# Sigmoid attention and a top-128 routed feed-forward on one core: small broadcasts on another queue, and several operations at another place in the order

## The chip, the core and the metric

The kernel runs on one core of a Trainium2 chip. The core has a matrix engine (TensorE, PE in the profile, with its weight loads as PEld), a vector engine (VectorE, DVE), an activation engine (ScalarE, ACT), GpSimd (POOL) and a SyncE (SP), which here only issues transfers. Each engine works through its own list of instructions in order. The metric is the device time of one execution in microseconds, as the median of several runs.

## What is computed

Attention first, for 8 batches and 12 heads, with 448 tokens and 64 values a head, all in float32. There is no softmax: each score passes a sigmoid.

```python
scores = (q @ k.T) / sqrt(64) - log(448)
x = sigmoid(scores) @ v             # heads side by side: 8 x 448 x 768
```

Then, in each batch, a gate picks 128 of the 448 tokens, and only these go through a feed-forward of width 1024. All other rows are copied.

```python
s = x[b] @ w_gate                   # one score a token
top = the 128 tokens with the highest s
h = relu(x[b, top] @ w1)            # w1 768 x 1024
out[b, top] = x[b, top] + sigmoid(s[top])[:, None] * (h @ w2)   # w2 1024 x 768
```

## The kernel before

**Stages and units.** Four heads of one batch are a group. There are 24 groups, three to a batch, and two groups make a stage, so there are 12 stages, s = 0 to 11, and a last one, s = 12, that holds only what is left over. A stage has seven units, n = 0 to 6; (s, n) below is unit n of stage s. `unit(s, n)` computes a block of scores on TensorE (line 214) and its sigmoid on ScalarE (line 222). `gap(s, n)` is called after each unit and fills the time with other work: the attention values of the stage before (line 249) in four parts, the first at (s-1, 6) and the others at (s, 0), (s, 1) and (s, 2), and after the third unit, pieces of the feed-forward (lines 382 and 392). TensorE runs this list in the written order.

**Order.** The order of instructions on every engine is that in which the Python code emits them; no scheduler moves them. `late` is a table from (s, n) to work that is emitted there, filled by `routed(b)`.

**Turning.** `turn(i)` (lines 189 to 196, VectorE) transposes the raw keys and queries of group i. It is emitted at (s, 5) for the first group of the next stage and at (s, 1) for the second group of its own. Raw buffers, kT and qT are two deep. `load(i)` fetches the raw data of a group and `load_v(s)` the values of a stage in eight transfers (lines 115 and 117), all on SyncE. The values' buffer is two deep too: `load_v(s+1)` is emitted at (s, 0), and its first transfer waits until TensorE has done with the values of stage s-1, at the end of (s, 2).

**Picking the tokens.** A batch b passes through these steps:
- `take` (line 264, VectorE) transposes the attention result out of PSUM into x_b, and `gate_part` (lines 272 and 275) multiplies by w_gate and sums.
- `gate(b)` (lines 288 to 307) adds up the scores into `total`, writes them to DRAM (`scores`) and reads them back into all 128 partitions (`rep`).
- `ranking(b)` (lines 315 and 318, then `place`) counts for each token how many others are above it, writes the counts (`ranks`) to DRAM, and reads them back to all partitions (`spot`).
- `choose(b)` (line 341 to 354, in `select`) compares `spot` with the partition's number and so finds which token stands at which place. The row numbers drive an indirect gather of the rows `xe` from DRAM (line 352, GpSimd).
- `follow(b)` transposes xe on TensorE (`turn_rows`, line 366) and queues three pieces of `ffn1` and three of `ffn2`. The last ffn2 piece scatters the rows to the output (line 398, GpSimd).
- `store(b)` writes x_b to DRAM in four transfers (line 281) and `copy_out(b)` copies all rows of the batch to the output (line 284), both on SyncE.

The small transfers scores, rep, ranks and spot are issued by GpSimd. For batch 0 the steps stand at: gate (2, 2), store (2, 4), ranking (3, 1), copy_out (3, 3), choose (4, 0), follow (4, 3). For batch 1: gate (3, 3), store (3, 4), ranking (4, 1), choose (5, 0), follow (5, 3). The other batches follow in the same pattern, two batches in three stages.

**Weights.** `WEIGHTS` says after which unit SyncE issues the loads of w1 (six transfers of 512 KB) and w2 (eight of 384 KB): five of w1 after (1, 5), the sixth and four of w2 after (2, 5), and the last four of w2 after (3, 1).

**A wait for a lane.** Each transfer signals one of eight semaphores of its queue in turn. In the built program a transfer therefore also waits for the one that used the same semaphore eight transfers earlier.

Of the kernel before, what the change touches and what calls it, by code (L numbers as in the profile page):

```python
# [10 lines left out]
I32 = mybir.dt.int32  # L11
AF = mybir.ActivationFunctionType
ALU = mybir.AluOpType
# [4 lines left out]
def kernel(  # L18
# [11 lines left out]
    nc = tc.nc  # L30

    B, H, S, Dh = q.shape
    D = H * Dh
    F = moe_w1.shape[1]
    CAP = moe_capacity
    P = 128
    TT = 32
    TB = S // TT
    NF = 3
# [4 lines left out]
    NU = 2 * NF + 1  # L44
    HP = H // 2
    KD = D // P
    KF = F // P
    ND = D // 3
# [7 lines left out]
    assert Dh == 2 * TT and TB == HK + 2 and S == TT * TB and H == 4 * NG and NQ == 2 * NS  # L56
    assert D == KD * P and F == KF * P and KF % 4 == 0 and 0 < CAP < S and D == HP * P

    out_flat = out.rearrange("b s d -> (b s) d")

    const = ctx.enter_context(tc.tile_pool(name="const", bufs=1))
    raw = ctx.enter_context(tc.tile_pool(name="raw", bufs=2))
# [5 lines left out]
    moe = ctx.enter_context(tc.tile_pool(name="moe", bufs=1))  # L68
# [7 lines left out]
    def banks(which):  # L76
        if which == "any":
            turns[1] ^= 1
            which = "psc" if turns[1] else "o"
        if which == "psc":  # L80
            return ps_sc.tile([P, 2, 512], F32, name="psc")
        if which == "o":
            turns[0] ^= 1
            which = turns[0]
        return ps_o[which].tile([P, 2, 512], F32, name=f"o{which}")
# [4 lines left out]
    def load(i):  # L90

        if i >= NQ:
            return
        raws[i] = [raw.tile([P, TB * Dh], F32, name=f"raw_{nm}") for nm in "kq"]
        for t, src in zip(raws[i], (k, q)):
            nc.sync.dma_start(
                out=t, in_=bass.AP(tensor=src.tensor, offset=src.offset + i * 4 * S * Dh,
                                   ap=[[TB * Dh, P], [1, TB * Dh]]))
# [19 lines left out]
                              in_=blocks(4 * (n // 2), HK + n % 2, 4, 1))  # L118


    WEIGHTS = {(1, NU - 2): (0, 5), (2, NU - 2): (5, 10), (3, 1): (10, KD + KF)}
    w1_sb = const.tile([P, KD, F], F32, name="w1_sb")
    w2_sb = const.tile([P, KF, D], F32, name="w2_sb")

# [99 lines left out]
    x_tiles, gate_parts, st = {}, {}, {}  # L224
# [43 lines left out]
    def gate_part(i):  # L268
        b, g = divmod(i, NG)
        for hp in range(2 * g, 2 * g + 2):  # L270
            tmp = moe.tile([P, TB, TT], F32, name="scr")
            nc.vector.tensor_tensor(  # L272
                out=tmp, in0=x_tiles[b][:, :, hp, :],
                in1=wg_b[:, hp:hp + 1, :].to_broadcast([P, TB, TT]), op=ALU.mult)
            nc.vector.tensor_reduce(out=gate_parts[b][:, :, hp], in_=tmp, axis=AX.X, op=ALU.add)  # L275
# [10 lines left out]
    def gate(b):  # L286

        nc.vector.tensor_reduce(out=gate_s[:, :TB], in_=gate_parts[b], axis=AX.X, op=ALU.add)
        by_dim = moe.tile([P, TT], F32, name="by_dim")
        nc.vector.transpose(by_dim, gate_s)  # L290
        parts = moe.tile([TT, 4, TT], F32, name="parts")
        for a in range(4):
            nc.vector.tensor_copy(parts[:, a], by_dim[a * TT:(a + 1) * TT])
        total = moe.tile([TT, TT], F32, name="total")
        nc.vector.tensor_reduce(out=total, in_=parts.rearrange("p a t -> p t a"), axis=AX.X,
                                op=ALU.add)
        scores = dram.tile([TB, TT], F32, name="scores")
        nc.gpsimd.dma_start(out=scores, in_=total[:TB])
        rep = moe.tile([P, S], F32, name="rep", bufs=2)
        nc.gpsimd.dma_start(out=rep, in_=bass.AP(tensor=scores.tensor, offset=scores.offset,  # L300
                                                 ap=[[0, P], [1, S]]))
        by_token = moe.tile([TT, TT], F32, name="by_token")
        nc.vector.transpose(by_token, total)
        for m in range(4):
            n = min(NC, TB - m * NC)
            nc.vector.tensor_copy(score[m * TT:(m + 1) * TT, :n],
                                  by_token[:, m * NC:m * NC + n])
        st[b]["rep"] = rep
# [13 lines left out]
    def place(b):  # L322

        nc.vector.tensor_add(place_s[:, :NC], above, level)
        by_col = moe.tile([P, TT], F32, name="by_col")
        nc.vector.transpose(by_col, place_s)
        ranks = dram.tile([P, TT], F32, name="ranks")
        nc.gpsimd.dma_start(out=ranks, in_=by_col)
        spot = moe.tile([P, 4, NC * TT], F32, name="spot")
        nc.gpsimd.dma_start(  # L330
            out=spot, in_=bass.AP(tensor=ranks.tensor, offset=ranks.offset,
                                  ap=[[0, P], [TT * TT, 4], [1, NC * TT]]))
        st[b]["spot"] = spot.rearrange("p m c -> p (m c)")[:, :S]

    def select(b, s0, n):

        picked = []
        for what in (number.rearrange("p r t -> p (r t)"), st[b]["rep"]):
            got = moe.tile([P, 1], F32, name="got", bufs=4)
            junk = moe.tile([P, S], F32, name="scr")  # L340
            nc.vector.scalar_tensor_tensor(
                out=junk[:n], in0=st[b]["spot"][:n], scalar=slots[s0][:n], in1=what[:n],
                op0=ALU.is_equal, op1=ALU.mult, accum_out=got[:n, 0:1])
            picked.append(got)
        row = moe.tile([P, 1], I32, name="row", bufs=2)
        nc.vector.tensor_copy(row[:n], picked[0][:n])
        idx = moe.tile([P, 1], I32, name="idx", bufs=2)
        nc.vector.tensor_scalar_add(idx[:n], picked[0][:n], float(b * S))
        gt = moe.tile([P, 1], F32, name="gate", bufs=2)
        nc.scalar.activation(gt[:n], picked[1][:n], AF.Sigmoid)  # L350
        xe = moe.tile([P, D], F32, name="xe", bufs=2)
        nc.gpsimd.indirect_dma_start(
            out=xe[:n], out_offset=None, in_=st[b]["x_d"][:, :],
            in_offset=bass.IndirectOffsetOnAxis(ap=row[:n, 0:1], axis=0))
        st[b].update(idx=idx, gate=gt, xe=xe)
# [31 lines left out]
    def ffn2(b, n, part, where):  # L387
        ps = banks(where)[:, 0]
        xe = st[b]["xe"]
        cols = slice(part * ND, (part + 1) * ND)  # L390
        for t in range(KF):
            nc.tensor.matmul(ps[:n, :ND], st[b]["hT"][:, t, :n], w2_sb[:, t, cols],  # L392
                             start=(t == 0), stop=(t == KF - 1))
        nc.vector.scalar_tensor_tensor(  # L394
            out=xe[:n, cols], in0=ps[:n, :ND], scalar=st[b]["gate"][:n, 0:1],
            in1=xe[:n, cols], op0=ALU.mult, op1=ALU.add)
        if part == D // ND - 1:
            nc.gpsimd.indirect_dma_start(
                out=out_flat[:, :],
                out_offset=bass.IndirectOffsetOnAxis(ap=st[b]["idx"][:n, 0:1], axis=0),  # L400
                in_=xe[:n], in_offset=None)


    ready = []

    def routed_groups(b, n):
        for f0 in range(0, KF, 3):
            ready.append((ffn1, (b, n, f0, min(f0 + 3, KF))))
        for part in range(D // ND):
            ready.append((ffn2, (b, n, part)))  # L410

    def go(where="o"):
        if ready:
            fn, args = ready.pop(0)
            fn(*args, where)

    late = {}

    def put(where, s, n, fn, *args):
        where.setdefault((s, n), []).append((fn, args))  # L420

    def due(where, s, n):
        for fn, args in where.pop((s, n), []):
            fn(*args)

    def routed(b):

        s = (NG * b + NG - 1) // 2 + 1
        put(late, s, 4, store, b)
        if s == NS:  # L430
            return
        put(late, s + 1, 1, ranking, b)
        put(late, s + 1, 3, copy_out, b)
        if s + 2 <= NS:
            put(late, s + 2, 0, choose, b)
            put(late, s + 2, 3, follow, b)

    def ranking(b):
# [13 lines left out]
    def gates(i):  # L452
        gate_part(i)
        b, g = divmod(i, NG)
        if g == NG - 1:
            st[b] = {}
            gate(b)

    def gap(s, n):
        if n < 3 and s > 0:  # L460
            values(s - 1, n + 1)
            if n == 2:
                turns[0] = 1
                gates(2 * s - 2)
        if 3 <= n < NU - 1:
            if not ready:
                due(late, s, n)
            go("any" if s == NS else "o")
            if n == NU - 2 and s < NS - 4 and len(ready) > 1:
                go()  # L470
        if n == NU - 1 and s < NS:
            values(s, 0)
        due(late, s, n)
        if n == 3 and s > 0:
            gates(2 * s - 1)

    def stream():
        for b in range(B):
# [13 lines left out]
        for s in range(NS):  # L492
            for n in range(NU):
# [7 lines left out]
                if n == NU - 2:  # L501
                    turn(2 * s + 2)
                    load(2 * s + 4)
                load_weights(*WEIGHTS.get((s, n), (0, 0)))

        for n in range(5):
            gap(NS, n)
# [50 lines left out]
```

## Time and profile before

| what | value |
|---|---|
| median of 3 runs (lowest to highest) | 477.78 us (475.13 to 478.36) |
| span of the profiled execution | 476.9 us |
| mean granted TensorE clock | 0.987 |
| busy DVE, ACT, POOL | 227.5, 185.1, 47.0 us |
| data moved | 72.74 MB, mean 153 GB/s |
| TensorE idle within 113.08 to 141.21 us, with clock | 28.13 - 23.07 = 5.06 us, clock 0.88 |

The profile names a transfer or operation by what it writes and reads, as in `rep<-scores`. An engine is busy while one of its instructions runs. The chain of waits goes back from the last instruction to whatever released each step. The table's last row comes from the busy times by stretch, for the stretch from the fourth unit of stage 4 to the end of its feed-forward pieces; the feed-forward of batch 0 lies in it.

### The profile page before, as it was taken

What the parts mean: (1) busy time and instruction counts of PE and PEld (TensorE: products, weight loads), DVE (VectorE), ACT (ScalarE), POOL (GpSimd) and SP (SyncE); (2) the same over time, 40 slices, a digit from 0 to 9 for tenths busy, and PEclk for the clock granted to TensorE, in tenths of its full rate; (3) what the DMA queues carried; (4) which work ended last, traced back from release to release, by engine and by line L of the source; (5) the groups of instructions that cost most, each with busy time, mean ns of one, the idle gap of its engine ahead of it and who ended that gap; (6) DMA issues with size and microseconds to landing.
All of it is one profiled execution on the core that took longest, in us unless ns stands there. A gap on an engine that the chain in (4) does not pass through costs nothing.

```text
span 476.9 us, 14574 instructions
## 1 busy us (share of the span) xinstructions
PE 457.0 (96%) x6582; PEld 299.7 (63%) x6582; DVE 227.5 (48%) x557; ACT 185.1 (39%) x245; POOL 47.0 (10%) x74
## 2 busy tenths in 40 slices
PE   8998989896999999999999999999999999999994
PEld 3473636353864684664774654755656738999993
DVE  4309087657322826666910844954454628540100
ACT  3856455653234425535344435455434520101010
POOL 9000000010000010001100011011010010220000
PEclk9999989998899999999999999999999999999999
DMA  8928688999912881697860892986822734722000
GB/s 267 206 80 216 241 194 198 265 356 177 313 36 93 184 180 42 143 232 170 200 238 3 184 183 57 271 147 138 263 69 34 148 97 72 211 60 67 34 0 33
DMA packets 118941, 72.74 MB, mean 153 GB/s; under 512 B 96288, under 2 KB 108768, under 8 KB 118624
## 3 DMA queue, kind: packets, MB, share of 16 engines
q1 hardware_dynamic: 115808, 61.35, 50.5%
q0 software_dynamic: 3072, 10.47, 9.7%
q8 instruction: 51, 0.84, 0.7%
q14 instruction: 10, 0.08, 0.0%
HBM read 57.51 MB, written 25.31 MB: 174 GB/s over the span
## 4 chain that ended last, share of the span: by engine, by line
PE 85%; issue 4%; DMA 4%; DVE 3%; ACT 1%; SPq 0%; POOLq 0%; DVEq 0%; ACTq 0%
PE o L249 24%; PE psc L214 24%; PE o L382 14%; PE o L392 12%; PE psc L392 4%; PE psc L382 2%; PE o L214 2%; DMA rep<-scores 1%; DMA w_sb<-in_moe_w_dram 1%; ACT attn L222 1%; PE o L490 1%; PE o L366 1%; DMA out_dram<-xe,idx 1%; DVE x_b L264 1%; DVE scr L318 1%
## 5 line engine op out<-in xcount | busy, mean ns | idle before, releaser
L222 ACT ACTIVATE attn<-psc,bias_s 128x896 f32<-128x896 f32 x156 | 148.7, 1004 | 121.7 <-PE psc L214 121.6
L214 PE MATMUL psc<-qT,kT 32*64 32x448 f32 x2496 | 150.0, 544 | 4.2 <-ACT attn L222 4.2
L249 PE MATMUL o<-attn,raw_v 32*64 32x448 f32 x2304 | 135.4, 537 | 1.1 <-ACT o L252 1.1
L214 PEld LDWEIGHTS psc<-qT,kT 32*64 32x64 f32 x2496 | 61.0, 132 | 63.3 <-issue 40.1
L249 PEld LDWEIGHTS o<-attn,raw_v 32*64 32x64 f32 x2304 | 61.2, 133 | 51.4 <-issue 42.4
L264 DVE STREAM_TRANSPOSE x_b<-o 128x448 f32<-128x448 f32 x48 | 26.9, 618 | 98.1 <-PE o L249 98.1
L382 PEld LDWEIGHTS o<-xeT,w_sb 128*128 128x128 f32 x576 | 67.3, 196 | 10.0 <-issue 5.7
L382 PE MATMUL o<-xeT,w_sb 128*128 128x128 f32 x576 | 69.8, 281 | 0.9 <-ACT xeT L372 0.9
L392 PE MATMUL o<-w_sb,hT 128*128 128x256 f32 x272 | 62.5, 383 | 1.2 <-DVE xe L394 1.2
L392 PEld LDWEIGHTS o<-w_sb,hT 128*128 128x128 f32 x272 | 50.5, 190 | 15.6 <-issue 5.1
L189 DVE STREAM_TRANSPOSE kT<-raw_k 128x384 f32<-128x384 f32 x48 | 24.7, 553 | 35.1 <-PE psc L214 27.5
L394 DVE SCALAR_TENSOR_TENSOR xe<-o,gate,xe 128x256 f32<-128x256 f32 x17 | 8.2, 484 | 55.3 <-PE o L392 55.1
L275 DVE TENSOR_REDUCE gate_p<-scr 128x14 f32<-128x448 f32 x48 | 29.8, 621 | 1.6
L272 DVE TENSOR_TENSOR scr<-x_b,wg_b 128x448 f32<-128x448 f32 x48 | 29.5, 614 | 1.0
L385 ACT ACTIVATE hT<-o 128x384 f32<-128x384 f32 (+1 forms) x20 | 9.1, 454 | 50.3 <-PE o L382 50.3
L315 DVE TENSOR_SCALAR_CACHE_REDUCE scr<-rep,score 128x448 f32<-128x448 f32 (+1 forms) x32 | 21.5, 673 | 13.6 <-DMA rep<-scores 12.8
L249 PE MATMUL o<-attn,raw_h 32*64 32x448 f32 x384 | 27.2, 535 | 0.0
L392 PE MATMUL psc<-w_sb,hT 128*128 128x256 f32 x112 | 25.4, 380 | 0.0
L196 DVE STREAM_TRANSPOSE qT<-raw_q 128x896 f32<-128x896 f32 x23 | 24.7, 1073 | 0.7 <-DMA raw_q<-in_q_dram 0.7
L392 PEld LDWEIGHTS psc<-w_sb,hT 128*128 128x128 f32 x112 | 21.0, 190 | 3.4 <-issue 0.7
L318 DVE SCALAR_TENSOR_TENSOR scr<-rep,score,earlier 128x448 f32<-128x448 f32 (+1 forms) x32 | 21.8, 682 | 1.4
L252 ACT ACTIVATE o<-bias_s 1x1 f32<-1x1 f32 x36 | 5.9, 165 | 39.5 <-PE o L249 22.2
(69 smaller groups left out, 219.7 us busy)
## 6 DMA issues: line engine op xcount, KB each, us to landing
raw_k<-in_k_dram SPq DMA_DIRECT2D x24, 448.0 KB, 5.3
raw_q<-in_q_dram SPq DMA_DIRECT2D x24, 448.0 KB, 5.3
x_d<-x_b SPq DMA_DIRECT2D x32, 336.0 KB, 7.7
out_dram<-x_d SPq DMA_DIRECT2D x8, 1344.0 KB, 8.2
raw_v<-in_v_dram SPq DMA_DIRECT2D x48, 192.0 KB, 5.0
w_sb<-in_moe_w_dram SPq DMA_DIRECT2D x6, 512.0 KB, 7.9
w_sb<-in_moe_w_dram SPq DMA_DIRECT2D x8, 384.0 KB, 6.9
spot<-ranks POOLq DMA_DIRECT2D x8, 256.0 KB, 5.8
```

The lines of the kernel that those rows point to most:

```text
L189: nc.vector.transpose(kT[i][:, e, :HK], sk[:, e, :HK].rearrange("p (m c) d -> p c m d", c=NF))
L196: nc.vector.transpose(qT[i], sq)
L214: nc.tensor.matmul(psc[h // 2][y * Dh:(y + 1) * Dh, h % 2, :S], kT[2 * s + x][d, e, r:r + 2, :].rearrange("d r t -> d (r t)"), qT[2 * s + ...
L222: nc.scalar.activation(a, psc[pr][:, :, :S], AF.Sigmoid, bias=bias_s, scale=QK_SCALE)
L249: nc.tensor.matmul(o[x][j * Dh:(j + 1) * Dh, pr, :S], w, a[rows, j, :], start=(n == 0 and c == 0), stop=(n == 3 and c == NF - 1))
L264: nc.vector.transpose(x_tiles[b][:, :, 2 * g + pr, :], outs[s][x][:, pr, :S].rearrange("p (r t) -> p r t", t=TT))
L272: nc.vector.tensor_tensor(out=tmp, in0=x_tiles[b][:, :, hp, :], in1=wg_b[:, hp:hp + 1, :].to_broadcast([P, TB, TT]), op=ALU.mult)
L275: nc.vector.tensor_reduce(out=gate_parts[b][:, :, hp], in_=tmp, axis=AX.X, op=ALU.add)
L315: nc.vector.tensor_scalar(out=junk[:n], in0=rep[:n], scalar1=own, scalar2=0.0, op0=ALU.is_gt, op1=ALU.add, accum_out=above[:n, c:c + 1])
L318: nc.vector.scalar_tensor_tensor(out=junk[:n], in0=rep[:n], scalar=own, in1=earlier[:n, c, :], op0=ALU.is_equal, op1=ALU.mult, accum_out=l ...
L382: nc.tensor.matmul(ps[:, f - f0, :n], w1_sb[:, t, f * P:(f + 1) * P], xeT[:, t // (KD // 2), t % (KD // 2), :n], start=(t == 0), stop=(t = ...
L392: nc.tensor.matmul(ps[:n, :ND], st[b]["hT"][:, t, :n], w2_sb[:, t, cols], start=(t == 0), stop=(t == KF - 1))
```

## The change

Five things are altered.

1. The four small transfers of `gate` and `place` (scores, rep, ranks, spot; 32 in all) go from GpSimd's queue to SyncE's. They are to keep GpSimd free for the gather and the scatter.
2. `choose(0)` moves from (4, 0) to (3, 3), ahead of the second `gate_part` there and of `gate(1)`, so that the first gather can start earlier. On VectorE it comes ahead of `gate_part` of group 5, `gate(1)` and `turn(8)`.
3. The weights come in two lots: w1 whole after (1, 5), w2 whole after (4, 3).
4. Small operations come later: `gate(b)` is put off to the third gap through the list `waiting`, behind whatever is emitted there, and `copy_out` goes from (s+1, 3) to (s+1, 4).
5. For the last batch the scatter is split: each of the three ffn2 pieces scatters its own 256 columns, with indices of its own. `idx` gets four buffers instead of two.

```diff
-    WEIGHTS = {(1, NU - 2): (0, 5), (2, NU - 2): (5, 10), (3, 1): (10, KD + KF)}
+    WEIGHTS = {(1, NU - 2): (0, KD), (4, NF): (KD, KD + KF)}
...
-        nc.gpsimd.dma_start(out=scores, in_=total[:TB])
+        nc.sync.dma_start(out=scores, in_=total[:TB])
...
-        nc.gpsimd.dma_start(out=rep, in_=bass.AP(tensor=scores.tensor, offset=scores.offset,
-                                                 ap=[[0, P], [1, S]]))
+        nc.sync.dma_start(out=rep, in_=bass.AP(tensor=scores.tensor, offset=scores.offset,
+                                               ap=[[0, P], [1, S]]))
...
-        nc.gpsimd.dma_start(out=ranks, in_=by_col)
+        nc.sync.dma_start(out=ranks, in_=by_col)
...
-        nc.gpsimd.dma_start(
+        nc.sync.dma_start(
             out=spot, in_=bass.AP(tensor=ranks.tensor, offset=ranks.offset,
...
-        idx = moe.tile([P, 1], I32, name="idx", bufs=2)
-        nc.vector.tensor_scalar_add(idx[:n], picked[0][:n], float(b * S))
+        idx = []
+        pieces = D // ND if b == B - 1 else 1
+        for m in range(pieces):
+            at = moe.tile([P, 1], I32, name="idx", bufs=4)
+            nc.vector.tensor_scalar(out=at[:n], in0=picked[0][:n], scalar1=float(pieces),
+                                    scalar2=float(pieces * b * S + m), op0=ALU.mult, op1=ALU.add)
+            idx.append(at)
...
-        if part == D // ND - 1:
+        if b == B - 1 or part == D // ND - 1:
+            pieces = D // ND if b == B - 1 else 1
             nc.gpsimd.indirect_dma_start(
-                out=out_flat[:, :],
-                out_offset=bass.IndirectOffsetOnAxis(ap=st[b]["idx"][:n, 0:1], axis=0),
-                in_=xe[:n], in_offset=None)
+                out=out.rearrange("b s (p c) -> (b s p) c", p=pieces),
+                out_offset=bass.IndirectOffsetOnAxis(ap=st[b]["idx"].pop(0)[:n, 0:1], axis=0),
+                in_=xe[:n, cols] if pieces > 1 else xe[:n], in_offset=None)
...
-        put(late, s + 1, 3, copy_out, b)
+        put(late, s + 1, 4, copy_out, b)
         if s + 2 <= NS:
-            put(late, s + 2, 0, choose, b)
+            put(late, *((s + 1, 3) if b == 0 else (s + 2, 0)), choose, b)
...
             st[b] = {}
-            gate(b)
+            waiting.append(b)
...
         if n == 3 and s > 0:
+            if waiting:
+                gate(waiting.pop())
             gates(2 * s - 1)
+            if waiting:
+                gate(waiting.pop())
```

TensorE's list of instructions is the same as before, in the same order. On SyncE, the small transfers of a batch stand in this order around stage 3 and 4: values of stage 4, raw data of group 9, ranks(0), spot(0), scores(1), rep(1), copy_out(0), the four stores of batch 1, raw data of group 10, values of stage 5, raw data of group 11, ranks(1), spot(1), the eight loads of w2.

More of the change, by code (lines that the diff above doesn't have):

```diff
@@ L57 @@
     assert D == KD * P and F == KF * P and KF % 4 == 0 and 0 < CAP < S and D == HP * P
-    out_flat = out.rearrange("b s d -> (b s) d")
     const = ctx.enter_context(tc.tile_pool(name="const", bufs=1))
@@ L396, in ffn2 @@
             in1=xe[:n, cols], op0=ALU.mult, op1=ALU.add)
-        if part == D // ND - 1:
+        if b == B - 1 or part == D // ND - 1:
+            pieces = D // ND if b == B - 1 else 1
             nc.gpsimd.indirect_dma_start(
-                out=out_flat[:, :],
-                out_offset=bass.IndirectOffsetOnAxis(ap=st[b]["idx"][:n, 0:1], axis=0),
-                in_=xe[:n], in_offset=None)
+                out=out.rearrange("b s (p c) -> (b s p) c", p=pieces),
+                out_offset=bass.IndirectOffsetOnAxis(ap=st[b]["idx"].pop(0)[:n, 0:1], axis=0),
+                in_=xe[:n, cols] if pieces > 1 else xe[:n], in_offset=None)
     ready = []
+    waiting = []
     def routed_groups(b, n):
```

## The prediction

> **What bounds the kernel now.** I read the busy shares first, then the waits of TensorE and of SyncE's queue, then the chain of waits and the timeline where TensorE stood still. The page says who is the bound:
>
> ```profile
> PE 457.0 (96%) x6582; PEld 299.7 (63%) x6582; DVE 227.5 (48%) x557; ACT 185.1 (39%) x245; POOL 47.0 (10%) x74
> ```
>
> TensorE is busy for 96% of the span and nothing else for half. So a wait of another engine costs time only if TensorE comes to wait, and an addition to its waits is paid in full, because its list is fixed. The waits by engine, first TensorE's, then SyncE's queue:
>
> ```profile
> PE o L366 <- DVE x_b L264: 4.2, 1, 4.2
> ...
> SPq L115 <- PE o L249: 110.0, 9, 24.3
> ```
>
> TensorE's longest wait is one of 4.2 us ahead of the first turning of rows. The second line shows that SyncE stands still at the loads of values in nearly every stage, until TensorE has used the old ones; whatever is behind them in that queue waits too. The chain of waits at the 4.2 us:
>
> ```profile
> 96.13 6.58 DMA w_sb<-in_moe_w_dram
> 102.71 6.79 DMA rep<-scores
> ...
> 117.24 1.53 PE o L366 x6
> 118.80 0.82 ACT xeT L372
> ...
> 119.66 5.94 PE o L382 x36
> ...
> 127.29 4.21 PE o L382 x36
> ...
> 136.06 3.46 PE o L392 x16
> ```
>
> Weights in flight held up scores(1) and rep(1). VectorE's ranking(1) waited for rep to 109.6, x_b's transposes were behind it, and TensorE wanted their bank. The 36 matmuls after the wait took 5.94 us, against 4.21 for the next 36.
>
> The timeline of the stretch that the change rearranges:
>
> ```profile
> 83.00 0.57 POOL L328 DMA_DIRECT2D ranks<-by_col  x1 [9.92 <-DVE by_col L326]
> 90.06 0.77 POOL L330 DMA_DIRECT2D spot<-ranks  x1 [6.49 <-DMA ranks<-by_col]
> ...
> 86.83 1.81 SPq L115 DMA_DIRECT2D raw_v<-in_v_dram  x4
> ...
> 96.91 1.04 DVE L189 STREAM_TRANSPOSE kT<-raw_k 128x384 f32<-128x384 f32 x2
> ...
> 98.07 1.07 DVE L196 STREAM_TRANSPOSE qT<-raw_q 128x896 f32<-128x896 f32 x1
> 99.06 0.65 DVE L341 SCALAR_TENSOR_TENSOR scr<-spot,slot,number 128x448 f32<-128x448 f32 x1
> ...
> 99.28 1.76 PE L214 MATMUL psc<-qT,kT 32*64 32x448 f32 x32
> ```
>
> GpSimd sent ranks(0) at 83.0, with nothing ahead of it. SyncE was then waiting at the values until 86.83. And turn(8) ended at 99.14, just in time for TensorE's first unit of stage 4 at 99.28: there is no slack.
>
> **What the Trainium skill says.** "DMA: Bandwidth & Descriptors", section "Queues, rings and completion order", says that each DMA engine consumes descriptors of one row in ring order, and takes turns between rows. A small transfer on SyncE's row thus stands behind the loads issued ahead of it, which one on GpSimd's row didn't. The trace fits: values of 32 KB landed 3.9 us after issue behind large ones (window 60 to 65 us), ranks in 1.8 us where the queues were quiet (from 380 us); no run here shows ranks on SyncE. "TensorE: Matmul & The Clock Gate", section "What's actually happening", halves the clock after an idle window of about 3.4 us. The trace agrees: 5.94 against 4.21 us above, and the clock was 0.88 on average from 113 to 141 us.
>
> **The change part by part.**
>
> *The first pick and ranks/spot on SyncE.* spot(0) now stands behind the values of stage 4. They start at 86.83, since TensorE's work up to there is unchanged. Eight loads of values and two raw loads took from 60.31 to 64.99 a stage earlier, 4.7 us, so ranks(0) is issued at about 91.7, not 83.0. It lies behind raw_q, which landed 4.3 to 4.8 us after its issue at these places, so near 96; at best it takes its fastest 1.7 us and lands at 93.4. SyncE may issue spot only then. Spot on GpSimd landed in 5.2 to 7.1 us; I take 5.2, so 101.3. At best it is as quick as the fastest rep, 3.6 us: 97.1. choose(0) waits for it on VectorE, and behind it are: choose itself 1.5 us (99.06 to 100.56), gate_part(5) 2.6 (91.66 to 94.26), gate(1) 2.6 (94.29 to 96.90), turn(8) 2.2 (96.91 to 99.14), 8.9 in all. TensorE's stage 4 then starts at 110.2 instead of 99.28: **+10.9 us**, at best 106.0, +6.7, and with ranks 2 us and spot 1 us slower some +14. The wait is long enough for the clock to drop: after the 4.2 us wait the six transposes took 1.53 us against 0.66 elsewhere and the 36 matmuls 1.7 too much, 2.6 together. I take **+2** (1 to 3).
>
> *The old wait.* With fewer weights in flight and rep(1) sent early against the delayed TensorE, ranking(1) ends before the values at (4, 2) do: total(1) near 107.3, scores 3 us (fastest 3.0), rep 4.3, so ranking from about 115 to 121; TensorE ends the values at about 124. The 4.2 us and the 2.6 of slow clock go, less a little: **-6.5** (-4 to -7).
>
> *w2 after (4, 3).* It is now the last in a long row on SyncE. From total(1) at 107.3: scores landed 110.4, rep and copy_out issued 111.6, four stores of x_d 14.4 us when a copy_out is in flight (at 201.38; others 10 to 16.7) to 126, raw data of group 10 4.5 (215.86 to 220.36) to 130.5, values and raw data under such load 7.6 (116.95 to 124.56) to 138, ranks(1) 4.4 to 142.5, spot 0.8. Eight loads of w2 at 0.45 us take 3.6, and one lands 7 us after issue (medians 6.9 and 7.9), so the last is there near 154; with 4.7 for the values near 151. I take 152. TensorE: stage 4 at 110.2, 2 for the clock, 13.8 to the turning of rows (99.28 to 113.08), then 117.24 to 136.06 less the slow clock, 16.2, so ffn2 could start at 142.2 and end at 145.7. It needs all eight tiles in this piece: **+6.5**, and 1 for the clock. At the best end (stores 10.5, values 4.7, ranks 1.7, landing 5.6) the tiles come by 141, at no cost; at the worst 11.
>
> *Last scatter.* One of 384 KB took 3.9 us in the median and 3.0 at the least; the last now carries a third. The three write one tensor and follow each other, but a piece takes 3.47 us, about as long as a scatter. **-1** (0 to -1.5).
>
> *Free.* Later stages have 16.8 us of TensorE work between the end of (s, 2) and (s+1, 0) (194.81 to 211.60), and the same chain of values, ranks and spot takes about 15. scores and rep there have half a stage. The raw loads, 10 us later behind the added waits, have a stage of 33 us. gate(b) behind ffn2's addition costs VectorE 0.5 us, and VectorE is 48% busy. More idx buffers take away 8.4 us of VectorE's waits; the longest, at 413.29, held no matmul, TensorE being busy throughout.
>
> Sum: 10.9 + 2 - 6.5 + 6.5 + 1 - 1 = +12.9, or about **490 us**.
>
> **The rivals.**
> - *w2 arrives in time.* Stores are quick without weights beside them. Then 10.9 + 2 - 6.5 - 1 = +5.4, 483 us. For it: 10.6 us for the stores at 65.73. Against it: a copy_out lies directly ahead.
> - *A draw.* spot at its best bound, full recovery: 6.7 + 1 - 7 - 1, about 477 us. For it: DMA carries 2 MB of weights less from 79 to 97 us. Against it: ring order, and two round trips through DRAM after 91.7.
> - *Faster.* The old wait goes and spot isn't late, because SyncE issues ranks sooner than I read: -6.7 - 1, 470 us. For it: this is all that TensorE lost there. Against it: the loads of values can't go before 86.83, and no slack is ahead of stage 4.
>
> **How the numbers follow.** Both stalls 0.55, w2 in time 0.22, draw 0.13, faster 0.10. The range from 475 to 499 takes in the first three, with the upper bounds that can be met together, and leaves out the fastest case and the sum of all worst ends (up to 505). Over 1% slower is above 482.6: the first case and more than half of the second, 0.69. Within 1%: the rest of the second and the draw, 0.21. Faster: 0.10.
>
> **What would show it.** Right: in the profile after, VectorE waits for spot before its first line of choose, TensorE has a wait for turn(8)'s qT or kT of about 11 us near 99 to 110, the wait at the first turning of rows is gone, and the first ffn2 piece waits for w_sb. Wrong: ranks(0) issued well before 91 us, spot(0) landed by 92, or w2 landed by 142. If the other stages changed length by over 1 us each, "free" was wrong.

## The result, and the profile after

The changed kernel takes 492.99 us in the median, against 477.16 us for the kernel before beside it: a ratio of 1.0336, with a 95% interval of 1.0295 to 1.0377. It is slower by 3.4%, about as forecast (490.0). Medians in this document are over all executions, while ratios leave out slow ones, more than 1.5% above the fastest of the same kernel, so the two can differ a little. The profiled executions have spans of 490.4 and 476.9 us, a difference of 13.5 us; the medians are 15.8 us apart. In the changed kernel's lines L213 is the block of scores, L221 its sigmoid, L248 the attention values, L340 the comparison in `choose`, L371 the turning of rows, L387 ffn1, L397 ffn2 and L404 the scatter.

The busy shares on the page of the kernel after:

```profile
PE 458.2 (93%) x6582; PEld 304.0 (62%) x6582; DVE 227.1 (46%) x559; ACT 184.8 (38%) x245; POOL 28.9 (6%) x44
```

TensorE has the same number of instructions and 1.2 us more busy time. So nearly all of the 13.5 us is idle time of TensorE. GpSimd's own work has shrunk, from 47.0 to 28.9 us, and GpSimd was never the bound. The waits of TensorE and of SyncE's queue in the kernel after (microseconds in total, how often, the longest):

```profile
PE psc L213 <- ACT attn L221: 16.1, 3, 13.3
PE o L397 <- DMA w_sb<-in_moe_w_dram: 3.7, 4, 2.9
PE psc L371 <- DMA xe<-x_d,row: 2.6, 1, 2.6
...
SPq L329 <- DMA ranks<-by_col: 25.5, 8, 4.1
```

The one long wait of before, 4.2 us for x_b, is gone. Three others have come: 13.3 us, 3.7 us, and 2.6 us. The last line is new to SyncE: its queue now stands still eight times for ranks to land, 25.5 us in all, and everything behind in its list does too. It also waits for the totals (62.6 us) and for scores to land (15.9 us). The chain of waits of the kernel after passes through the first two:

```profile
84.21 0.33 SPq L114
...
89.25 4.92 DMA ranks<-by_col
94.19 4.48 DMA spot<-ranks
98.76 0.70 DVE scr L340 x2
...
100.22 0.20 ACT gate L355
...
135.56 7.41 DMA spot<-ranks
142.99 7.69 DMA w_sb<-in_moe_w_dram
```

Spot stands in it twice, both times with ranks and the values' loads right ahead (ranks(1) at 130.87, 4.67 us). The first time they hold up `choose(0)`. The second time they hold up the loads of w2, which stand behind them on SyncE. The timeline of the kernel after shows who waited:

```profile
98.76 0.68 DVE L340 SCALAR_TENSOR_TENSOR scr<-spot,slot,number 128x448 f32<-128x448 f32 x1 [9.75 <-DMA spot<-ranks]
...
100.22 0.20 ACT L355 ACTIVATE gate<-got 128x1 f32<-128x1 f32 x1 [12.62 <-DVE scr L340]
...
103.17 3.43 PE L213 MATMUL psc<-qT,kT 32*64 32x448 f32 x26 [13.33 <-ACT attn L221]
...
106.62 1.07 DVE L195 STREAM_TRANSPOSE qT<-raw_q 128x896 f32<-128x896 f32 x1
...
123.81 0.85 PE L371 MATMUL o<-iden,xe 128*128 128x128 f32 x6
...
144.06 4.49 PE L397 MATMUL o<-w_sb,hT 128*128 128x256 f32 x10 [2.90 <-DMA w_sb<-in_moe_w_dram]
```

VectorE waited 9.75 us for spot. But the engine that stopped TensorE was ScalarE: `choose(0)` ends with a sigmoid of the 128 picked scores (L355), which stands in ScalarE's list ahead of sigmoids of the attention scores. ScalarE stood still for 12.62 us, the banks of PSUM (the memory that TensorE writes its results to) were not emptied, and TensorE stopped at (3, 6), the unit before stage 4. The turning of rows at 123.81 has no wait, and the first piece of ffn2 waits for w2, whose eight loads SyncE issued from 135.99 on.

Where the 13.5 us are, by the distance between the two profiles at the same instruction:

| stretch | us |
|---|---|
| up to the values of (3, 2), from a clock granted otherwise at the start and at 66 to 72 us | -2.6 |
| the stop at (3, 6) with the slow matmuls after it | +13.2 |
| the old wait at the turning of rows and its slow matmuls | -5.5 |
| ffn2 waits for w2 | +6.85 |
| the middle of the run | -1.0 |
| near the end: rows of batch 6 come late | +4.5 |
| from the start of the last scatter to the end | -2.0 |

The first line is most likely not the change's doing. The six matmuls that open the kernel took 5.49 us before and 4.28 after, the 26 near 67 us 3.20 and 2.27, and in the other kernels' profiles below the loads of stage 4's values, which follow from there, start anywhere from 84.2 to 88.4 us. Without this line the profiles differ by 16.1 us, close to the medians.

The +4.5 lies where I had written "free". The timelines near the end, first two lines of the kernel before, then the kernel after:

```profile
379.47 0.53 SPq L284 DMA_DIRECT2D out_dram<-x_d  x1
...
408.90 1.03 POOL L398 DMA_INDIRECT out_dram<-xe,idx  x1 [0.30 <-issue]
```

```profile
415.32 0.34 SPq L297 DMA_DIRECT2D scores<-total  x1
...
417.13 0.54 SPq L283 DMA_DIRECT2D out_dram<-x_d  x1
...
425.22 0.99 POOL L404 DMA_INDIRECT out_dram<-xe,idx  x1 [54.35 <-DVE scr L317]
431.33 0.97 POOL L357 DMA_INDIRECT xe<-x_d,row  x1 [5.13 <-DVE xe L399]
...
436.63 0.84 PE L371 MATMUL psc<-iden,xe 128*128 128x128 f32 x6 [2.62 <-DMA xe<-x_d,row]
437.31 5.31 PE L397 MATMUL o<-w_sb,hT 128*128 128x256 f32 x16
```

`copy_out(6)` at (12, 4) now stands on SyncE behind scores(7) and rep(7), which wait for the attention to end. So it went out at 417.13, where the kernel before has it at 379.47. A scatter into the same output came at 425.22 (before 408.90), although VectorE had finished its rows at 417.14. The copy's landing isn't recorded, so that the scatter waited for it is inferred here; the run with an earlier copy, below, bears it out. The gather of the next rows behind that on GpSimd came at 431.33 instead of 414.09. TensorE waited 2.62 us for them, and the next ffn2 piece took 5.31 us, against 3.62 elsewhere.

### The profile page after: what moved, and what is told of

The parts are those of the page before. It is cut to its first block, busy times and chain, and to the rows that moved or that the text cites. A ratio compares the mean times of both kernels' runs of the same rounds, so it can differ in the third digit from the quotient of the medians.

```text
span 490.4 us, 14570 instructions
## 1 busy us (share of the span) xinstructions
PE 458.2 (93%) x6582; PEld 304.0 (62%) x6582; DVE 227.1 (46%) x559; ACT 184.8 (38%) x245; POOL 28.9 (6%) x44
## 4 chain that ended last, share of the span: by engine, by line
PE 85%; DMA 10%; ACT 2%; DVE 1%; issue 1%; SPq 0%; POOLq 0%; DVEq 0%; ACTq 0%
PE o L248 26%; PE psc L213 24%; PE o L387 13%; PE o L397 12%; PE psc L397 4%; PE psc L387 3%; DMA spot<-ranks 2%; DMA raw_v<-in_v_dram 2%; PE o L213 2%; DMA ranks<-by_col 2%; ACT attn L221 2%; DMA w_sb<-in_moe_w_dram 2%; DMA xe<-x_d,row 1%; PE o L371 1%; DMA raw_k<-in_k_dram 1%
## 5 line engine op out<-in xcount | busy, mean ns | idle before, releaser
L221 ACT ACTIVATE attn<-psc,bias_s 128x896 f32<-128x896 f32 x156 | 148.7, 1004 | 126.8 <-PE psc L213 126.7
L213 PE MATMUL psc<-qT,kT 32*64 32x448 f32 x2496 | 149.9, 545 | 16.4 <-ACT attn L221 16.1
L248 PE MATMUL o<-attn,raw_v 32*64 32x448 f32 x2304 | 134.3, 535 | 1.1 <-ACT o L251 1.1
L213 PEld LDWEIGHTS psc<-qT,kT 32*64 32x64 f32 x2496 | 63.2, 132 | 71.8 <-issue 35.7
L248 PEld LDWEIGHTS o<-attn,raw_v 32*64 32x64 f32 x2304 | 63.7, 132 | 49.0 <-issue 35.5
L387 PEld LDWEIGHTS o<-xeT,w_sb 128*128 128x128 f32 x576 | 65.6, 192 | 10.6 <-issue 5.7
L397 PE MATMUL o<-w_sb,hT 128*128 128x256 f32 x272 | 67.1, 400 | 3.7 <-DMA w_sb<-in_moe_w_dram 3.7
L387 PE MATMUL o<-xeT,w_sb 128*128 128x128 f32 x576 | 68.2, 277 | 1.8 <-ACT xeT L377 1.8
L397 PEld LDWEIGHTS o<-w_sb,hT 128*128 128x128 f32 x272 | 51.7, 197 | 21.4 <-issue 8.9
L248 PE MATMUL o<-attn,raw_h 32*64 32x448 f32 x384 | 26.8, 535 | 0.0
L397 PE MATMUL psc<-w_sb,hT 128*128 128x256 f32 x112 | 25.4, 380 | 0.0
L314 DVE TENSOR_SCALAR_CACHE_REDUCE scr<-rep,score 128x448 f32<-128x448 f32 (+1 forms) x32 | 21.5, 671 | 3.7 <-DMA rep<-scores 2.8
L397 PEld LDWEIGHTS psc<-w_sb,hT 128*128 128x128 f32 x112 | 21.0, 190 | 3.4 <-issue 0.7
L357 POOL DMA_INDIRECT xe<-x_d,row x8 | 8.1, 1014 | 246.6 <-DVE idx L351 88.7
```

The source lines that it names most:

```text
L213: nc.tensor.matmul(psc[h // 2][y * Dh:(y + 1) * Dh, h % 2, :S], kT[2 * s + x][d, e, r:r + 2, :].rearrange("d r t -> d (r t)"), qT[2 * s + ...
L221: nc.scalar.activation(a, psc[pr][:, :, :S], AF.Sigmoid, bias=bias_s, scale=QK_SCALE)
L248: nc.tensor.matmul(o[x][j * Dh:(j + 1) * Dh, pr, :S], w, a[rows, j, :], start=(n == 0 and c == 0), stop=(n == 3 and c == NF - 1))
L314: nc.vector.tensor_scalar(out=junk[:n], in0=rep[:n], scalar1=own, scalar2=0.0, op0=ALU.is_gt, op1=ALU.add, accum_out=above[:n, c:c + 1])
L387: nc.tensor.matmul(ps[:, f - f0, :n], w1_sb[:, t, f * P:(f + 1) * P], xeT[:, t // (KD // 2), t % (KD // 2), :n], start=(t == 0), stop=(t = ...
```

## The experiments

### The queue alone

Only the four small transfers go to SyncE; all else is as before.

```diff
 # in the kernel before
-        nc.gpsimd.dma_start(out=scores, in_=total[:TB])
+        nc.sync.dma_start(out=scores, in_=total[:TB])
...
 # rep, ranks and spot likewise
```

> The kernel before with the four small transfers on SyncE's queue, and nothing else. My theory: choose(0) at (4, 0) doesn't stop TensorE, but scores(1) and rep(1) stand behind spot(0), four loads of w2 and copy_out(0), so ranking(1) ends 6 to 8 us later than before and the wait at the first turning of rows grows from 4.2 to about 10.5 us; the last picks are untouched, because copy_out(6) is ahead of scores(7). About 484 us. Rival (the queue matters only where choose was moved up): 477.5 us.

It took 490.33 us, a ratio of 1.0253 (1.0199 to 1.0306): the queue alone costs 12.6 us. Its chain of waits, then TensorE's longest wait:

```profile
106.75 10.83 DMA scores<-total
...
PE o L366 <- DVE x_b L264: 9.5, 1, 9.5
```

With `choose` at its old place the loss moves: `choose(0)` waited for spot to 108.38, and scores(1), 1,792 bytes, was issued at 106.75 instead of 96.23 and took 10.83 us to land, instead of 5.96, behind spot(0), four loads of w2 and copy_out(0). The wait at the turning of rows grew from 4.2 to 9.5 us. I had foreseen a loss, but only half of it. Most of the other half came through ScalarE:

```profile
110.98 3.31 PE L214 MATMUL psc<-qT,kT 32*64 32x448 f32 x26 [1.89 <-ACT attn L222]
```

The picks' sigmoid waited 4.20 us for spot here too, so `choose(0)` at (4, 0) did stop TensorE, at (4, 2). With the slow matmuls after it that stop cost 4.6 us, by the distance to the kernel before.

### All but the queue

The changed kernel with the four small transfers back on GpSimd.

```diff
 # in the kernel after
-        nc.sync.dma_start(out=scores, in_=total[:TB])
+        nc.gpsimd.dma_start(out=scores, in_=total[:TB])
...
 # rep, ranks and spot likewise
```

> The changed kernel with scores, rep, ranks and spot back on GpSimd's queue; choose(0) early, two lots, late copy_out and the split scatter stay. My theory (standing behind other transfers in SyncE's list is the root of all three waits): ranks(0) goes at 80 us, spot(0) lands near 90, the first wait shrinks from 13.3 to about 3 us; w2 is issued near 115 and in time; copy_out(6) isn't blocked. 493 - 10 - 6.9 - 4.5 = about 472 us, faster than the kernel before. Rival (the new places of the operations cost the time, on whichever queue): 483 us or more.

It took 477.76 us, a ratio of 0.9999 (0.9979 to 1.0019), between the two expectations. There is no wait for w2 and none for xe, with the same lots of weights, the same place of `copy_out` and the same place of `choose(0)`. The loads of w2 begin at 123.28, not 135.99. So the loss as a whole comes from the queue. The timeline shows why the rest isn't faster than before:

```profile
97.75 2.69 PE L213 MATMUL psc<-qT,kT 32*64 32x448 f32 x18 [7.05 <-ACT attn L221]
```

Even on GpSimd, spot(0), issued at 85.92 and landed 7.33 us later, comes late for `choose(0)` at (3, 3), and the picks' sigmoid stops TensorE for 7.05 us, in place of 1.4. That gives back the old wait, which is gone.

### The first pick at its old place

```diff
 # in the kernel after
-            put(late, *((s + 1, 3) if b == 0 else (s + 2, 0)), choose, b)
+            put(late, s + 2, 0, choose, b)
```

> The changed kernel with choose(0) back at (4, 0); all else as changed. My theory (three separate waits of TensorE: the early choose 13.2 us, the late w2 6.9 us, the late copy_out 4.5 us): the 13.3 us wait near 90 us goes, but SyncE's row of transfers ahead of w2 doesn't move up with TensorE, so that TensorE reaches the first ffn2 piece near 127 us and w2 is there only near 143: that wait grows from 6.9 to about 13 us. Time about 486 us. Rival (the place of choose is the whole loss, the rest follows from it): about 478 us.

It took 487.12 us, 1.0178 (1.0124 to 1.0232), one microsecond from the first expectation. The 13.3 us wait for ScalarE is gone (the longest is 1.4 us again), TensorE comes to ffn2 earlier, and waits there instead:

```profile
PE o L397 <- DMA w_sb<-in_moe_w_dram: 9.6, 3, 9.1
```

w2 is issued at 134.40 here and at 135.99 in the kernel after. The two waits lie one behind the other against the same late queue, so of the 13.2 us of the first stop only 5.9 are gained. Counted as in the table above, the late w2 costs 13.0 us here instead of 6.85, as expected.

### Only the picks' sigmoid later

`choose(0)` stays at (3, 3), but its sigmoid is emitted at (4, 0). This separates the ScalarE path, which the profile shows, from the VectorE path, which the prediction named.

```diff
 # in the kernel after
-        nc.scalar.activation(gt[:n], picked[1][:n], AF.Sigmoid)
+        if b == 0:
+            put(late, 4, 0, nc.scalar.activation, gt[:n], picked[1][:n], AF.Sigmoid)
+        else:
+            nc.scalar.activation(gt[:n], picked[1][:n], AF.Sigmoid)
```

> The changed kernel, but the sigmoid of the gate of batch 0 (on ScalarE) is emitted at (4, 0) instead of within choose(0); VectorE's part of choose stays at (3, 3). My theory (two chains behind spot(0) end almost together: ScalarE's sigmoid ahead of the attention sigmoids stops TensorE at (3, 5), and turn(8) behind choose on VectorE would stop it at (4, 0) anyway): the wait for ScalarE near 90 us falls to its old 1.4 us, a wait of about 10 us for turn(8) appears at (4, 0), and the time falls by 2 to 3 us only, to about 490.5 us. Rival A (ScalarE alone carries the wait): 481 us. Rival B (VectorE alone, as the prediction had it): 493 us.

It took 492.27 us, 1.0316 (1.0261 to 1.0371), only 0.7 us below the kernel after, where I expected 2 to 3. ScalarE's wait falls back to 1.4 us, and this one takes its place (the stop of the kernel after is at (3, 6), not at (3, 5) as the expectation says):

```profile
PE psc L213 <- DVE qT L195: 9.9, 1, 9.9
```

So the path that the prediction named, spot to `choose(0)` to `turn(8)`, is real and costs within about a microsecond of the other: from the values of (3, 2) to the turning of rows this version loses 0.9 us against the kernel after. In the kernel after it is hidden behind ScalarE's.

### The weights in three lots, as before

```diff
 # in the kernel after
-    WEIGHTS = {(1, NU - 2): (0, KD), (4, NF): (KD, KD + KF)}
+    WEIGHTS = {(1, NU - 2): (0, 5), (2, NU - 2): (5, 10), (3, 1): (10, KD + KF)}
```

> The changed kernel with the weights in three lots as before. My theory: the wait for w2 (6.9 us) goes, but 2 MB of weights are then in flight ahead of the values of stage 4 and of ranks(0) in SyncE's row, so that spot(0) comes up to 5 us later and the first wait grows by as much: 488 to 493 us, and no wait for w_sb. Rival (the w2 wait is a pure loss and nothing depends on it): 486 us.

It took 494.82 us, 1.035 (1.0309 to 1.0392), above my 488 to 493. The wait for w2 is gone, as expected, but the first one grew by 8 us to 21.5, not by 5. The values' loads, issued behind the weights, took SyncE until 94.2 us, ranks(0) went out at 96.58 and spot(0) took 7.00 us. So the two lots are not what makes the changed kernel slow: on this queue, weights ahead of the small transfers (494.82 us) or behind them (492.99) cost about the same.

### The copy earlier

```diff
 # in the kernel after
-        put(late, s + 1, 4, copy_out, b)
+        put(late, s + 1, 3, copy_out, b)
```

> The changed kernel with copy_out back at (s+1, 3). My theory: copy_out(6) is then ahead of scores(7) and rep(7) in SyncE's list, is issued near 390 us instead of 417, the scatter of batch 4 no longer waits for it, and the gather of batch 6 doesn't wait for that scatter: the 2.6 us wait of TensorE for xe near 434 us and the slow clock after it go, 4.5 us, so about 488.5 us. Rival (the gather is late for another reason, its own queue or indices): 493 us.

It took 491.23 us, 1.0261 (1.0219 to 1.0303), between the two expectations. The wait for xe near the end is gone: copy_out(6) was issued at 401.12, ahead of scores(7). The scatter started at 421.84, right behind the addition on VectorE that it needs (421.08, 0.48 us). But the first wait grew to 15.3 us and the one for w2 to 4.1, since copy_out(0) now goes out at 96.53, right behind spot(0), and copy_out(1) at 136.59, right ahead of w2:

```profile
137.46 10.63 SPq L130 DMA_DIRECT2D w_sb<-in_moe_w_dram  x8
```

Spot(0) beside the first took 6.54 us to land instead of 4.48, and the issue of w2 behind the second took 10.63 us instead of 7.33.

### The split scatter alone

The kernel before with the last scatter in three (the edit of `select` and `ffn2` above).

```diff
 # in the kernel before
-        if part == D // ND - 1:
+        if b == B - 1 or part == D // ND - 1:
```

> The kernel before with the split scatter of the last batch (and its indices) alone. My theory: the tail from the start of the last scatter to the end falls from 6.1 to about 4.2 us and nothing else moves: about 475.5 us, ratio 0.996. Rival (three scatters on one tensor wait for each other and take the gain back): 477.5 us.

It took 477.82 us, 1.0007 (0.9983 to 1.003): no gain. From the start of the last scatter to the end of the span: 6.1 us before, 6.2 with the split alone, 4.7 with the queue alone and the scatter whole, 4.1 after. So most of the 2.0 us saved at the tail come with the small transfers leaving GpSimd; the split adds 0.6 us once they have left, and nothing while they are there. Why GpSimd ends sooner then, no run settles.

### GpSimd's queue and the old place

Both edits at once: small transfers back on GpSimd, `choose(0)` back at (4, 0). Of the change only the lots of weights, the later small operations and the split remain.

```diff
 # in the kernel after
-        nc.sync.dma_start(out=scores, in_=total[:TB])
+        nc.gpsimd.dma_start(out=scores, in_=total[:TB])
...
-            put(late, *((s + 1, 3) if b == 0 else (s + 2, 0)), choose, b)
+            put(late, s + 2, 0, choose, b)
```

> The changed kernel with the four small transfers on GpSimd's queue and choose(0) at (4, 0); two lots, late copy_out and split scatter stay. My theory (the early choose still cost 5.7 us and slow clock on GpSimd's queue; the two lots take away the old wait for rep(1), since no weights are in flight at (3, 1)): no wait near 90 us beyond 1.4 us, little or none at the first turning of rows, w2 in time: about 470 us, 1.5% below the kernel before. Rival (w2 after (4, 3) comes too late once TensorE is early, or rep(1) is still late): 474 to 477 us.

It took 477.5 us, 1.0006 (0.998 to 1.0033): the 470 of the first expectation was not met. Single executions of this version spread from 471.79 to 480.44 us, and the profiled one was the shortest, so the same kernel was profiled once more.

> The kernel of the run with small transfers on GpSimd and choose(0) at (4, 0) once more, for a second profile, since its first profile spans 470.0 us and its timed runs lie mostly between 475 and 480 us. My theory: in most executions the last tiles of w2 land a few us after TensorE wants them (in the profiled one the wait was 0.2 us), so a wait for w_sb of 2 to 6 us shows. Rival: all waits as in the first profile, and a lower clock alone makes the difference.

That execution took 474.91 us. It had no wait for w2, and the old wait was back ("PE o L371" waiting for x_b, 3.8 us). Both expectations of it were wrong: taking the last four w2 loads out of the way of scores(1) does not reliably remove the old wait.

### The weights ahead of stage 3

The kernel before, with all weights issued ahead of stage 3.

```diff
 # in the kernel before
-    WEIGHTS = {(1, NU - 2): (0, 5), (2, NU - 2): (5, 10), (3, 1): (10, KD + KF)}
+    WEIGHTS = {(1, NU - 2): (0, 10), (2, NU - 2): (10, KD + KF)}
```

> The kernel before with nothing changed but the places of the weights: w1 and four tiles of w2 after (1, 5), the last four tiles after (2, 5), none in stage 3. My theory (the old 4.2 us wait and its slow clock come from the weights in flight beside scores(1) and rep(1), and w2 after (4, 3) was only just in time): rep(1) lands near 104 instead of 109.6 us, the wait at the first turning of rows falls below 1 us, w2 is never waited for, about 471 us, ratio 0.986. Rival (the extra transfers in stages 1 and 2 delay rep(0), ranks(0) or the values as much): 477 us.

Its median is 480.39 us, against 477.42 for the kernel before beside it; the ratio of 1.0013 (0.9982 to 1.0043) leaves out 13 of its 22 executions, all above 480 us. So it is no faster, and the 471 us that I expected were not met. Again its profiled execution, at 473.17 us with a wait of only 0.7 us at the turning of rows, was near the low end, and the kernel was profiled once more.

> The kernel with the weights ahead of stage 3 once more, for a second profile: its first one spans 471.4 us, while most of its timed executions took 478 to 481 us. My theory: in these the transfers of weights, values and stores run slower at some place, and TensorE waits there (at the first turning of rows, or for the raw data of a stage), 4 to 8 us more than in the first profile. Rival: the waits are those of the first profile, and only the granted clock is lower, by about 0.01 of 475 us.

That one took 482.03 us. The timeline of this second profile:

```profile
94.45 1.31 SPq L284 DMA_DIRECT2D out_dram<-x_d  x1
95.86 16.25 SPq L281 DMA_DIRECT2D x_d<-x_b  x4
...
97.78 0.53 POOL L298 DMA_DIRECT2D scores<-total  x1 [6.18 <-DVE by_token L303]
105.61 0.56 POOL L300 DMA_DIRECT2D rep<-scores  x1 [7.30 <-issue]
...
118.94 1.51 PE L366 MATMUL o<-iden,xe 128*128 128x128 f32 x6 [4.30 <-DVE x_b L264]
```

No weights are in flight here, and scores(1) still took over 7 us to let rep(1) go. What is in flight is copy_out(0) and the stores of batch 1. As the first expectation has it, TensorE waits at the turning of rows, 4.3 us instead of 0.7. Of the 8.9 us between the two profiles, about half arise from the values of (3, 2) to ffn2, and 3.3 us before.

### The copy and the stores out of the way as well

```diff
 # in the kernel before, with the weights ahead of stage 3
-        put(late, s, 4, store, b)
+        put(late, *((4, 2) if b == 1 else (s, 4)), store, b)
...
-        put(late, s + 1, 3, copy_out, b)
+        put(late, *((4, 2) if b == 0 else (s + 1, 3)), copy_out, b)
```

> The kernel before with all weights loaded ahead of stage 3, as in the run with the weights ahead of stage 3, and in addition the copy of batch 0 and the stores of batch 1 put at (4, 2), so that neither is in flight beside scores(1) and rep(1). Theory A (weights, copy and stores together held up rep(1)): rep(1) has landed by about 102 us, TensorE's wait at the first turning of rows is under 1 us and the 36 matmuls after it take about 4.3 us; the median falls by 4 to 6 us, to about 472, a ratio of 0.987 to 0.991. Rival B (the wait goes, but the stores, now issued from about 119 us, are landed late for the gather of batch 1, or the copy of batch 0 late for its scatter, and TensorE waits there instead): 476 to 479. Rival C (rep(1) is slow for another reason): the wait of about 4 us stays, 477 to 481.

It took 474.85 us, against 476.67 for the kernel before beside it: a ratio of 0.9952 (0.9933 to 0.9971). One of its 22 executions took 1,206 us; it is not in the ratio, and its cause is not known. The timeline:

```profile
95.37 0.53 POOL L298 DMA_DIRECT2D scores<-total  x1 [3.78 <-DVE by_token L303]
100.67 0.56 POOL L300 DMA_DIRECT2D rep<-scores  x1 [4.76 <-issue]
...
104.18 0.68 DVE L315 TENSOR_SCALAR_CACHE_REDUCE scr<-rep,score 128x448 f32<-128x448 f32 x1 [2.33 <-DMA rep<-scores]
...
114.00 0.84 PE L366 MATMUL o<-iden,xe 128*128 128x128 f32 x6
116.61 4.29 PE L382 MATMUL o<-xeT,w_sb 128*128 128x128 f32 x36 [1.76 <-ACT xeT L372]
```

rep(1) lands 3.4 us after its issue, where it took 6.8 before and 5.6 in the second profile above, and the ranking starts at 104.18, against 109.61 before. The turning of rows at 114.00 has no wait, and the 36 matmuls take 4.29 us instead of 5.94. The copy and the stores go out from 121.03 on. This is the one version that is faster than the kernel before, by 0.5%; in the profiles the gain is 4.7 us and in the medians 1.8, since the profiled execution of before (478.73 us) lies above its median and that of this version (473.99) below. The wait went as theory A has it, but the median fell by less than half of its 4 to 6 us, and where the rest went is open. Rivals B and C fall in this profile: neither the later stores nor the later copy made TensorE wait, and rep(1) was not slow. Since raw loads also move forward when the stores leave, the share of each of the three transfers is not separated.

## Why the prediction was right, point by point

- **The first stall** (10.9 and 2 for the clock). Measured 13.2. Ranks went out 5.0 us after the start of the values' loads (forecast 4.9), took 4.92 us (4.3) and spot 4.48 (5.2); `choose(0)` began 14.55 us after those loads (14.5). The place was half right: the wait for turn(8) that was to show it did not appear. "turn(8) ended at 99.14, just in time" made me look only at what stands behind the wait on VectorE. `choose` also emits a ScalarE instruction, and that one stopped TensorE earlier, at (3, 6). The qT of `turn(8)` was done at 107.69, and TensorE, already late, came to stage 4 at 109.50 without a wait for it. The later sigmoid in the experiment shows that both paths stop TensorE by nearly the same amount. That they do is luck: the number was right for a reason that was only the second to bind.
- **The old wait** (-6.5). Measured -5.5. It went because TensorE came later, as argued. That the weights alone held up rep(1) was too narrow: with no weights in flight the wait still came in one of two profiles, and with the copy of batch 0 and the stores of batch 1 moved as well it was gone.
- **w2 after (4, 3)** (+6.5 and 1). Measured +6.85. The forecast row of transfers is the one in the trace; the last tile landed at 150.7, against 152.
- **The last scatter** (-1). Measured -2.0, but the step failed: the split alone gives nothing. The emptier GpSimd queue gives 1.4 us, and the split 0.6 on top of it.
- **"Free"** failed. I checked the later stages' ranks and spot, and not what stands behind a small transfer on SyncE once `copy_out` is one unit later. copy_out(6) behind scores(7) cost 4.5 us. In the profiles the low early part (-2.6) and a middle shorter by 1.0 nearly cancel it, which is luck: 13.5 us against the forecast 12.9. In the medians it shows, with 15.8.
- **The rivals.** "w2 arrives in time" fell to the wait at ffn2; "a draw" and "faster" to ranks(0) at 89.25, which is 5.0 us after the values' loads, and to the two trips through DRAM behind it. But the faster rival named the right prize: with the old wait removed by other means, there is something to gain.

## What to carry to other kernels

A small transfer that waits for another engine should not share an in-order queue with bulk loads, as the 12.6 us show: it waits for their turn, and they wait for its semaphores. Before moving an operation that may wait, list what stands behind it on every engine that it has an instruction on, the smallest included. And a wait that is removed is worth only the distance to the next one, so search for what is late behind it, and compare several executions before believing one good profile.

## What the runs showed of the hardware

- **The issuing queue.** The Trainium skill, "DMA: Bandwidth & Descriptors", section "Issuing engines are not separate DMA queues", says that starting transfers from several engines saves only the time to start them, "which is usually small relative to the DMA itself". Here the choice of the issuing engine alone was worth 12.6 us. Part of it is that a queue issues in order and waits in order: with the queue alone moved, rep(1) was issued 14.9 us later than before, and some 10.5 of these had passed when scores(1) was issued. The rest is its landing, 10.83 us for 1,792 bytes instead of 5.96. That fits the ring order that the prediction names, but the load on the DMA engines at that moment is not separated from it. No run put the small transfers on a third queue without bulk loads.
- **The clock after short waits.** The same skill, "TensorE: Matmul & The Clock Gate", section "What's actually happening", puts the drop after an idle window of about 3.4 us. Here shorter waits were sometimes enough. After 2.62 us sixteen matmuls of ffn2 took 5.31 us instead of 3.62, with a mean granted clock of 0.68. After 1.40 us at (3, 6) 26 matmuls took 3.40 us in the fastest version, with a clock of 0.50 from 94.0 to 97.4 us; in the kernel before they took 2.27 us after the same wait, at full clock. After 1.76 us 36 matmuls took 4.29 us, as they do without a wait. So the length of one wait did not foretell the clock in these runs.
